# Pacing GpSimd's preparation steps by an estimate, and reordering the two products in each slot, in a fused attention and mixture kernel

## The chip, the cores and the metric

One core of one Trainium2 chip. The time is the device time of one execution in microseconds; the kernel before was run three times, with a median of 1210.46 us (1207.51 to 1210.76). The profile is of one more execution (1209.25 us by the same clock, 1207.5 us from its first to its last recorded instruction). TensorE's granted clock was full in it. All data are fp32.

## The reference: decayed linear attention, then four weighted two-layer experts

```python
# attention: batch 4, heads 8, seq 768, head_dim 64, in blocks of 64
for b in range(nb):
    qb, kb, vb = (q[:, :, sl], k[:, :, sl], v[:, :, sl])
    intra = np.einsum('bhic,bhjc->bhij', qb, kb) * Dmask[None]
    intra = np.einsum('bhij,bhjd->bhid', intra, vb)
    inter = np.einsum('bhid,bhde->bhie', qb * lam_pow[None], kv_state)
    out[:, :, sl] = intra + inter
    ...                                   # kv_state decays and takes in the block
# (B,H,S,D) -> x of (3072, 512); experts: E 4, F 1024
p = domain_probs / (domain_probs.sum(-1, keepdims=True) + 1e-09)
for e in range(E):
    h = np.maximum(x @ w1[e], 0.0)
    out += p[:, e:e + 1] * (h @ w2[e])
```

## The kernel before

Tokens come in 3 groups of 1024, each with 4 experts: 12 units (g, e). Both matrix products of a unit are done by a fast scheme with 7 outer products (`M1` to `M7`) in place of 8, and the first product x @ w1 by a second level of 7 inner products within each. The sums and differences of weight blocks (`S1` to `S4`) and of x blocks (`T1` to `T4`) that this needs are made ahead of time, mostly on GpSimd, stored in device memory (`w1_ops`, `x_ops`, `w2_sums`, `w2_ops`), and read back in the order of use. In the last group the second product is nested too (`nested_product`). While unit n does its second product, unit n+1 does its first product, and the attention of the next group is worked in between.

All instructions of all engines are issued in program order by this one Python program, and each engine runs its own in that order, waiting for data. SyncE (`nc.sync`) issues nearly all DMA transfers, also in order: a store that waits for its data holds back the loads behind it. So where in the program a preparation step, its store or a load is put decides what it can hold up. The preparation steps are closures in a list, taken one at a time:

```python
    chores, stores, older, made = [], [], [], set()

    def pump():
        for f in older:
            f()
        older[:] = stores
        stores.clear()
        if chores:
            chores.pop(0)()

    def until(what):
        while what not in made:
            pump()

    def inner(eng, what, to, blk, ops, at):          # 4 sums of 128x256, then their stores
        ...
            tt(eng, b[name], b[x], b[y], op)
        stores.append(lambda: (
            nc.sync.dma_start(out=to[:, 0], in_=blk[:, 0, 0:256]),
            nc.sync.dma_start(out=to[:, 1:5], in_=s[:]),
            nc.sync.dma_start(out=to[:, 5:7], in_=blk[:, 1].rearrange("p (a f) -> p a f", a=2)),
            made.add(what),
        ))

    def weight_steps(block, total, ready):           # block: loads; total: 2 sums of 128x512; ready: inner
        return [
            lambda: (block("A11", 0, 0), block("A21", 1, 0), block("A22", 1, 1)), nothing, nothing,
            lambda: ready("M1"),
            lambda: total("S1", "A21", "A22", ALU.add), lambda: ready("M5"),
            ...
        ]
```

The reads. `feed` fetches the operands of a first product (two buffers each), `feed2` the weights of a second product (a pool of six tiles, two for each product):

```python
    def feed(g, e, m):
        ...
        until(("x", g, m))
        until(("w1", e, m))
        xs = stream.tile([P, 7, 256], FP32, name="xs_in", tag="x")
        nc.sync.dma_start(out=xs[:], in_=x_ops[g, MS.index(m)])          # L633
        ws = stream.tile([P, 7, 256], FP32, name="ws_in", tag="w")
        nc.sync.dma_start(out=ws[:], in_=w1_ops[e, MS.index(m)])         # L635
        ...

    def first_product(g, e, m, blocks, tags):        # tags: PSUM banks g1, g3
        while (g, e, m) not in fed:
            pump()
        ...
        def inner(i):
            t = tags[0] if i in ("M1", "M6", "M5", "M3") else tags[1]
            ...
            for j in range(2):
                nc.tensor.matmul(...)                # L706: pg
            at, begins = READ[i]                     # then VectorE (or ScalarE) reads the bank
            ...
        return [lambda i=i: inner(i) for i in INNER] + [lambda: finished(g, e, m, blocks, new)]
        # INNER = ("M1", "M7", "M6", "M4", "M5", "M2", "M3")
```

`second_product` gives four parts (L760, tile q, each read by VectorE into `acc`) and a closing step; `nested_product` gives seven inner ones (L931, tile pq) and a closing step, with the pairs of banks q01/q02 and q11/q12 in turn. In the trace every matmul of the source stands as two matmul instructions.

The first expert's products on the first group are done directly (`direct_product`, L1021) with blocks still on chip, and the operands of the second expert's are made on the spot by `own(m)`: `own_x` on VectorE, `own_w1` on GpSimd, and a store of both (L1000). Then the main loop:

```python
    for at, (g, e) in enumerate(units):
        if (g, e) == (0, 1) or (g, e) == (0, 2):
            chores.extend(prepare_w2(e + 1) + prepare_w1((e + 2) % E))
        ...
        for i in range(7):
            for _ in range(2 if at + i == 0 else 1):
                if fill2:
                    feed2(*fill2.pop(0))
            ...
            if nested:
                order = [a[0:2], b[0:2], a[2:4], b[2:4], a[4:6], b[4:6], a[6:8], b[6:8]]
            else:
                order = [a[0:2], b[0:1], a[2:4], b[1:2], a[4:6], b[2:3], a[6:8], b[3:5]]
            for x, part in enumerate(order):         # a: first product of the next unit, b: second of this
                for f in part:
                    if f:
                        f()
                now[0] += 1
                ...
                if x == 0 and at * 7 + i >= 6 and fill:
                    feed(*fill.pop(0))
                ...                                  # at x 5 and some x 2: a step of the attention
                if x % (2 if g == 0 else 3) == 0:
                    pump()
```

## Time and profile before

| view | value |
|---|---|
| time, median of three runs | 1210.46 us |
| span of the profiled execution | 1207.5 us |
| TensorE matmul / weight load busy | 1187.3 / 1028.4 us |
| VectorE / ScalarE / GpSimd busy | 792.4 / 262.1 / 635.0 us |
| device memory traffic over the span | 262 GB/s |
| TensorE idle, 87 to 100 us | 2.95 us |
| TensorE idle, 400 to 896 us | 0.20 us |
| waits of SyncE for GpSimd, at L159 and L231 | 36.0 and 32.0 us |

Engines are called PE (TensorE matmul), PEld (its weight loads), DVE (VectorE), ACT (ScalarE), POOL (GpSimd) and SP (SyncE); SPq is the issuing of DMA by SyncE. "L706" is line 706 of the kernel; L94 is the helper that records every two-operand sum, so there the tile tells the sums apart. The chain that ended last is followed back from the last instruction, at each step to what released it. Matmul ends are modelled, so a short stall can stand inside "busy"; it then shows as a longer piece in the chain. A window's row gives its length, then for each engine the busy time and the number of instructions, then the clock, the DMA share and the rate.

### The profile page before, as it was taken

The page shows a single profiled execution, that of the slowest core. Times are in us where ns is not written, and L with a number is a line of the kernel's source. Part 1 is how long each engine was busy: PE and PEld are TensorE (multiplying, and loading weights), DVE is VectorE, ACT ScalarE, POOL GpSimd, SP SyncE. Part 2 cuts the span into 40 slices and gives each one's busy share as a digit, 9 for nine tenths or more (in the row PEclk, how much of TensorE's full clock was granted, in tenths as well). Part 3 has the DMA queues.
Part 4 walks back from the last instruction along what each step waited for, and adds up shares of the span by engine and source line. Part 5 has one row for each costly group of instructions (what it writes and reads, how often), then busy time and mean ns, then how long its engine had stood idle before and what let it go on. Part 6 is the DMA issues. An engine that isn't in the chain of part 4 may idle for free.

```text
span 1207.5 us, 17884 instructions
## 1 busy us (share of the span) xinstructions
PE 1187.3 (98%) x6593; PEld 1028.4 (85%) x6593; DVE 792.4 (66%) x1313; ACT 262.1 (22%) x476; POOL 635.0 (53%) x600
## 2 busy tenths in 40 slices
PE   7999999999999999999999999999999999999998
PEld 6887888888888888888888888888888888888877
DVE  5597687478467746746765774764665667777774
ACT  3322122112212211311221120120143241241132
POOL 4664258376366900025534746405665764873873
PEclk9999999999999999999999999999999999999999
DMA  9668479999999976679987998988987667566542
GB/s 234 186 217 293 171 250 330 366 332 349 334 328 344 306 233 197 225 238 291 299 284 239 298 326 309 304 311 259 320 297 249 226 216 260 205 248 211 203 172 72
DMA packets 227448, 317.94 MB, mean 263 GB/s; under 512 B 91649, under 2 KB 168865, under 8 KB 227361
## 3 DMA queue, kind: packets, MB, share of 16 engines
q1 hardware_dynamic: 219920, 314.63, 77.1%
q10 hardware_dynamic: 7440, 2.17, 0.8%
q8 instruction: 52, 0.85, 0.3%
q14 instruction: 36, 0.29, 0.1%
HBM read 231.40 MB, written 85.34 MB: 262 GB/s over the span
## 4 chain that ended last, share of the span: by engine, by line
PE 92%; DVE 3%; DMA 2%; SPq 2%; issue 1%; ACT 0%; DVEq 0%
PE pg L706 38%; PE q L760 30%; PE pq L931 13%; PE pM L1021 3%; PE op L488 2%; PE sp L460 2%; DMA ws_in<-w_ops 1%; PE op L483 1%; DVE m L94 1%; SPq L115 1%; PE kp L437 1%; PE qp L437 1%; PE op L496 1%; DVE hS L94 1%; PE pM L901 1%
## 5 line engine op out<-in xcount | busy, mean ns | idle before, releaser
L706 PE MATMUL pg<-xs_in,ws_in 128*128 128x256 f32 x1960 | 473.2, 382 | 1.4 <-DMA ws_in<-w_ops 1.0
L706 PEld LDWEIGHTS pg<-xs_in,ws_in 128*128 128x128 f32 x1960 | 368.7, 190 | 57.9 <-DVE m L94 5.7
L94 DVE TENSOR_TENSOR m<-pg,m 128x512 f32<-128x512 f32 x451 | 307.7, 688 | 132.2 <-PE pg L706 124.1
L760 PE MATMUL q<-w2t,hS 128*128 128x256 f32 x1024 | 242.6, 380 | 0.0
L760 PEld LDWEIGHTS q<-w2t,hS 128*128 128x128 f32 x1024 | 194.3, 190 | 26.3
L776 DVE SCALAR_TENSOR_TENSOR acc<-q,gate,acc 128x256 f32<-128x256 f32 x192 | 92.5, 482 | 155.8 <-PE q L760 155.5
L760 PE MATMUL q<-w2t,m 128*128 128x256 f32 x768 | 181.9, 380 | 2.1 <-DMA w2t<-in_moe_w_dram 2.1
L760 PEld LDWEIGHTS q<-w2t,m 128*128 128x128 f32 x768 | 145.7, 190 | 22.1 <-ACT m L1033 2.5
L718 ACT ACTIVATE m<-m 128x512 f32<-128x512 f32 x132 | 82.9, 630 | 346.7 <-DVE m L94 308.7
L94 POOL TENSOR_TENSOR kn<-kn,s_decay 128x512 f32<-128x512 f32 x20 | 22.6, 1132 | 204.1 <-PE kp L437 161.8
L94 POOL TENSOR_TENSOR m<-m,xT 128x512 f32<-128x512 f32 x64 | 81.2, 1286 | 73.9 <-ACT m L718 60.4
L94 DVE TENSOR_TENSOR sums<-pq,sums 128x256 f32<-128x256 f32 x154 | 64.6, 422 | 46.8 <-PE pq L931 43.1
L931 PE MATMUL pq<-acc,w2t 128*128 128x256 f32 x352 | 86.7, 380 | 0.0
L714 ACT COPY m<-pg 128x512 f32<-128x512 f32 x88 | 51.2, 585 | 142.9 <-PE pg L706 142.8
L94 DVE TENSOR_TENSOR m<-m,m 128x512 f32<-128x512 f32 x96 | 79.3, 832 | 0.0
L931 PEld LDWEIGHTS pq<-acc,w2t 128*128 128x128 f32 x352 | 66.9, 190 | 9.4 <-issue 0.6
L94 POOL TENSOR_TENSOR ops<-w2b 128x256 f32<-128x256 f32 x24 | 18.3, 783 | 104.2 <-DMA w2b<-in_moe_w_dram 92.9
L653 ACT ACTIVATE m<-m 128x512 f32<-128x512 f32 x48 | 30.3, 631 | 147.0 <-DVE m L94 147.0
L94 POOL TENSOR_TENSOR acc<-hT,hT 128x512 f32<-128x512 f32 x32 | 40.2, 1269 | 30.7 <-PE pq L931 21.3
L94 DVE TENSOR_TENSOR hS<-m,m 128x512 f32<-128x512 f32 x64 | 52.5, 824 | 5.6 <-ACT m L718 5.6
L94 POOL TENSOR_TENSOR w2o<-w2b 128x512 f32<-128x512 f32 x32 | 42.2, 1341 | 13.0 <-DMA w2b<-in_moe_w_dram 11.2
L94 POOL TENSOR_TENSOR acc<-hT,acc 128x512 f32<-128x512 f32 x32 | 40.7, 1270 | 7.4 <-PE pq L931 5.4
(126 smaller groups left out, 1321.1 us busy)
## 6 DMA issues: line engine op xcount, KB each, us to landing
xs_in<-x_ops SPq DMA_DIRECT2D x70, 896.0 KB, 4.9
ws_in<-w_ops SPq DMA_DIRECT2D x70, 896.0 KB, 8.2
w2t<-w_ops SPq DMA_DIRECT2D x66, 256.0 KB, 6.6
w2t<-w_sums SPq DMA_DIRECT2D x64, 256.0 KB, 5.0
w_ops<-ops SPq DMA_DIRECT2D x28, 512.0 KB, 5.7
w2t<-in_moe_w_dram SPq DMA_DIRECT2D x48, 256.0 KB, 4.2
x_ops<-ops SPq DMA_DIRECT2D x17, 512.0 KB, 6.2
w2b<-in_moe_w_dram SPq DMA_DIRECT2D x32, 256.0 KB, 5.7
```

Of the source, the lines that this page charges most:

```text
L94: eng.tensor_tensor(out=o, in0=a, in1=b, op=op)
L437: nc.tensor.transpose(out=x[:, ac * C:(ac + 1) * C], in_=y[:, 2 * ac:2 * ac + 2].rearrange("p r d -> p (r d)"), identity=ident[:],)
L460: nc.tensor.matmul(out=sp[r][:, ac * C:(ac + 1) * C], lhsT=hc(kT)[half[r], ac], rhs=hc(qT)[half[r], ac], start=True, stop=True,)
L488: nc.tensor.matmul(out=op[r][half[x], a * C:(a + 1) * C], lhsT=vn[:, 4 * r + 2 * a + x], rhs=hc(st[r])[:, 2 * a + x], start=(first and a = ...
L653: nc.scalar.activation(out=o[:], in_=o[:], func=AF.Relu)
L706: nc.tensor.matmul(out=p[:, j * 256:(j + 1) * 256], lhsT=ws[i][:, j * P:(j + 1) * P], rhs=xs[i], start=(fresh and j == 0), stop=True, skip ...
L714: nc.scalar.copy(out=new[at][:], in_=p[:])
L718: nc.scalar.activation(out=new[at][:], in_=new[at][:], func=AF.Relu)
L760: nc.tensor.matmul(out=p[:, s * DH:(s + 1) * DH], lhsT=h[A_OF[m]][:, c * 256 + s * P:c * 256 + (s + 1) * P], rhs=fed2[g, e, m][uu][:, c], ...
L776: nc.vector.scalar_tensor_tensor(out=o, in0=x, scalar=w, in1=o, op0=ALU.mult, op1=ALU.add)
L931: nc.tensor.matmul(out=p[:, 0:256], lhsT=fed3[e, m, x // 2][:, x % 2, c * P:(c + 1) * P], rhs=b[B_OF[i]][:, c * 256:(c + 1) * 256], start= ...
L1021: nc.tensor.matmul(out=p[:, s * 256:(s + 1) * 256], lhsT=a[c][:, f:f + P], rhs=b[:, c, j * 256:(j + 1) * 256], start=(s == 0 and c == 0), ...
```

## The change

It does four things. A running estimate of GpSimd's backlog is kept in slots (`now` counts slots, every sum on GpSimd adds its elements / 480), a preparation step begins when the estimate says that the last one has been worked off (`free`), and its store is put into SyncE's queue two slots after the estimate says that its sums are done, instead of two pumps later. The pump is called in every slot, with a factor for each group (`PACE`), and also in the prologue; where something must exist at once, steps are forced. Within a slot pair, the second product's part goes ahead of the first product's. And the weights of the first two second products are asked for before the last direct product; as that keeps the weights one outer product further ahead, each `feed2` later asks for the product after the next. Before the first chunk of a group overwrites the x tile, the x operands of the group before it are forced (`until`). Results have a list of their own and are stored at the next pump.

```diff
     def tt(eng, o, a, b, op):
         eng.tensor_tensor(out=o, in0=a, in1=b, op=op)
+        if eng is nc.gpsimd:
+            busy[0] = max(busy[0], now[0]) + math.prod(o.shape[1:]) / 480
+    now, busy, free = [0], [0.0], [0.0]
...
+    chores, queue, results, made = [], [], [], set()
+    LEFT = 1
+    def store(f):
+        queue.append((busy[0] + 2, f))
+    def pump(pace=1.0, force=False):
+        while results:
+            results.pop(0)()
+        begins = chores and (force or free[0] <= now[0])
+        while queue and (force or queue[0][0] <= now[0] or begins and len(queue) > LEFT):
+            queue.pop(0)[1]()
+        if begins:
+            begin = free[0] = max(free[0], now[0] - 1)
+            was = max(busy[0], now[0])
             chores.pop(0)()
+            free[0] = max(free[0], begin + max(pace * (busy[0] - was), 1))
+    def pause(n):
+        def step():
+            free[0] = max(free[0], now[0] + n)
+        return step
     def until(what):
         while what not in made:
-            pump()
+            pump(force=True)
...                                       # every stores.append(...) becomes store(...)
-            lambda: (block("A11", 0, 0), block("A21", 1, 0), block("A22", 1, 1)), nothing, nothing,
+            lambda: (block("A11", 0, 0), block("A21", 1, 0), block("A22", 1, 1)), pause(6),
...
             def end(n=n):
+                if n == g * CPG:
+                    for m in MS:
+                        until(("x", g - 1, m))
                 values(n, ("s0", "s1"))
...                                       # prologue: now[0] += 1; pump() after every part
+    chores.extend((*prepare_w2(1), *raws, pause(4), mine["M1"], sum_own("S1", "A21", "A22", ALU.add)))
     for m in SEQ0[2:]:
+        if m == SEQ0[-1]:
+            for _ in range(2):
+                feed2(*fill2.pop(0))
         for x, f in enumerate(direct_product(0, m, blocks, ("g1", "g3", "q01", "q02", "q11", "q12"))):
...
+    start, w1_steps = now[0], prepare_w1(2)
+    def pause_till(i, x):
+        def step():
+            free[0] = max(free[0], start + 8 * i + x)
+        return step
     chores.extend((
-        mine["M5"], sum_own("S2", "S1", "A11"), nothing, nothing,
-        mine["M6"], sum_own("S3", "A11", "A21"), nothing, nothing,
+        mine["M5"], sum_own("S2", "S1", "A11"),
+        pause_till(0, 4), mine["M6"], sum_own("S3", "A11", "A21"),
...                                       # M2, M7, M3, M4 likewise at (1, 4) to (4, 4)
+    PACE = 1.0, 1.4, 1.0
     for at, (g, e) in enumerate(units):
-        if (g, e) == (0, 1) or (g, e) == (0, 2):
-            chores.extend(prepare_w2(e + 1) + prepare_w1((e + 2) % E))
+        if at == 0:
+            chores.extend(prepare_w2(2) + prepare_w1(3) + prepare_w2(3) + prepare_w1(0))
...
-            for _ in range(2 if at + i == 0 else 1):
-                if fill2:
-                    feed2(*fill2.pop(0))
+            if fill2:
+                feed2(*fill2.pop(0))
...
-            if nested:
-                order = [a[0:2], b[0:2], a[2:4], b[2:4], a[4:6], b[4:6], a[6:8], b[6:8]]
+            if not ahead:
+                order = [[], b[0:2], [], b[2:4], [], b[4:6], [], b[6:8]]
+            elif nested:
+                order = [b[0:2], a[0:2], b[2:4], a[2:4], b[4:6], a[4:6], b[6:8], a[6:8]]
             else:
-                order = [a[0:2], b[0:1], a[2:4], b[1:2], a[4:6], b[2:3], a[6:8], b[3:5]]
+                order = [b[0:1], a[0:2], b[1:2], a[2:4], b[2:3], a[4:6], b[3:5], a[6:8]]
...
-                if x % (2 if g == 0 else 3) == 0:
-                    pump()
+                pump(PACE[g])
```

## The prediction

> **What bounds the kernel now.** I read the page first: the shares of the engines, then the windows of the trace, then the chain that ended last in the windows where TensorE was not full, then TensorE's waits.
>
> ```profile
> PE 1187.3 (98%) x6593; PEld 1028.4 (85%) x6593; DVE 792.4 (66%) x1313; ACT 262.1 (22%) x476; POOL 635.0 (53%) x600
> ```
>
> TensorE is the bound: idle 1207.5 - 1187.3 = 20.2 us in all. The next engine, VectorE, has 66%, GpSimd 53%. So the paced engine, GpSimd, isn't the limit; its work can only hurt by being late or by getting in the way of something. Where do the 20 us lie? The windows (length, then busy us of PE, PEld, DVE, ACT, POOL, clock, DMA share, GB/s) say:
>
> ```profile
> 87.00:100.00 13.00, 10.05 (x45) 7.97 (x44) 12.80 (x17) 4.40 (x8) 7.47 (x7) 1.00 0.55 195
> 165.00:175.00 10.00, 8.76 (x42) 7.39 (x40) 9.57 (x15) 1.89 (x3) 5.94 (x6) 1.00 0.55 191
> 217.00:259.00 42.00, 41.05 (x254) 34.99 (x253) 25.16 (x40) 5.85 (x11) 26.80 (x25) 1.00 0.97 342
> 400.00:896.00 496.00, 495.80 (x2668) 432.98 (x2667) 309.45 (x502) 92.45 (x162) 208.70 (x223) 1.00 0.84 278
> 896.00:1151.00 255.00, 254.78 (x1166) 220.05 (x1165) 174.74 (x310) 70.13 (x133) 169.54 (x136) 1.00 0.64 229
> ```
>
> The reader is to see that between 87 and 1151 us only 2.95 + 1.24 + 0.95 + 0.20 + 0.22 = 5.6 us are idle. The rest is before 60 us (6.0 in the first 20 us, 1.85 in the next 40) and after 1151 us (6.8 of the span); neither the first loads nor the closing additions are touched by the diff.
>
> The largest hole, at 93.7 to 99.1 us, is explained by the chain in order of time (start, us, what):
>
> ```profile
> 88.35 1.75 DVE ops L94 x2
> ...
> 91.85 0.33 SPq L1000
> ...
> 94.63 4.34 DMA w2t<-in_moe_w_dram
> 98.97 0.14 issue
> 99.11 1.10 PE q L760 x4
> ```
>
> VectorE makes the x operands of `own("M1")` until 91.8; SyncE's queue stands in order behind the store of them (L1000); only then the weights of the first second product are asked for, they land at 98.97, and TensorE starts L760 at 99.11. The direct products (L1021) ended at 93.7. From there to the end of that first L760 part, at 101.07, TensorE did 16 matmul instructions; eight take 1.73 us elsewhere in the chain, so 3.46 us of work took 7.4: **3.9 us lost**.
>
> A second loss is hidden in "busy". In the last group of tokens the chain shows, product after product, the same pattern:
>
> ```profile
> 929.76 0.86 PE pg L706 x4
> 930.62 0.86 PE pq L931 x4
> 931.49 1.92 PE pg L706 x8
> 933.40 1.73 PE pq L931 x8
> ```
>
> The eight L706 matmuls that open a product take 1.81 to 1.98 us, not 1.73. They write bank g1, which the last inner product (M3) of the product before also used, and VectorE must first empty it: 0.69 us for 128x512 from PSUM. Between the two stand only the 0.86 us of the half part of L931. TensorE's weight-load waits in 900 to 1150 us name it:
>
> ```profile
> PEld pg L706 <- DVE m L94: 4.9, 14, 0.6
> ```
>
> From 907.15 to 1140.23 us the chain has 19 such periods, mean 12.27 us; 56 instructions at 1.73/8 us would be 12.09. So 0.18 x 19 = **3.4 us** are lost there.
>
> **What the Trainium skill says.** "Perfetto Trace Analysis", section Identifying the Most-Contended Engine, warns that matmul busy is no measure of headroom, and points to the busy share of weight loads. This trace agrees: 98% against 85%, and the 3.4 us above are nearly invisible as idle time (0.22 us). The same page, Matmuls, wants independent groups to rotate through PSUM banks so that emptying one overlaps the next; here L931 rotates over pairs of banks and doesn't stall, while L706 returns to g1 and does. "GPSIMD Engine Reference", section 3.1, has 4497 ns for a two-input add of 2048 fp32 per partition; an estimate from that, a quarter, is 1.12 us for 512. The trace has 1.27 to 1.47 us for the 128x512 groups of GpSimd and 0.73 to 0.93 for 128x256. The measurement decides.
>
> **The change part by part.** One slot of the main loop: a product takes 12.95 us for 8 slots (711.18 to 724.13 in the chain), 1.62 us each.
>
> 1. *The estimate.* 512 elements / 480 = 1.07 slots = 1.73 us; 256 give 0.86 us. That is 20 to 35% above the measured 512 forms and about right for 256. So the pace is a little slower than GpSimd can go and should never pile work up.
> 2. *Pace.* Before, in group 0, a step every 2 slots; now one begins when the last is taken as done. A `ready` step has 4 x 256 and a `total` 2 x 512, both 1024/480 = 2.13 slots, against 2 before. In group 1: 1.4 x 2.13 = 3.0 against 8/3 = 2.67. Groups are thus paced much as before; pauses and plain loads are cheaper. Counting the queue through slot by slot, the deadlines hold: weights of expert 2, "M1", are stored about 10 slots ahead of the slot that asks for them, the last of expert 0 more than 50. The tight spots are the first two `own` steps (both forced just ahead of their product), the forced `until` at the fifth product of the first unit (about 8 slots of GpSimd work queued at once), and x of group 1, M5, forced by one step. I expect no TensorE idle time from this part, 0 +- 2 us.
> 3. *Stores by time, not two pumps later.* SyncE waited 36.0 us for GpSimd at L159 and 32.0 at L231, with the weights of the next product behind it. That caused TensorE's two waits for ws_in (1.0 us). Some of it goes: I take 0.5 us.
> 4. *First second-product weights asked for ahead.* The four w2t transfers now stand in SyncE's queue before the direct M4 and the `own("M1")` store. The 4.34 us of landing lie beside 7 us of L1021. The 2.09 us wait goes, and so do the 0.86 us (0.22 + 0.64) in which TensorE waits for VectorE to empty g1 and g3, since the L760 part now comes first. `own("M1")` also moves behind the direct M4 in VectorE's order, so its 3.5 us (88.3 to 91.8) no longer delay the emptying of the direct banks. But VectorE is 12.80 of 13.00 us busy there, and its backlog (the hS sums) must be worked off. Of 3.9 us I count 3.0.
> 5. *Second product first.* Cyclically the order of parts is the same, a b a b; what moves is the seam. Old: the last a (0.86), the last b, then the next a. In the last group that b was the half part, 0.86 us; new, the next product's full part, 1.73 us, lies between, longer than 0.69 us plus hand-over. So 3.0 of the 3.4 us go. b doesn't stall in its place, as it alternates banks, except at unit seams (three, 0.2 us each). In groups 0 and 1 the old gap was already 1.73 us: nothing. At the last seam (1151 us) the wait of 0.96 us before L931 at 1153.47 shrinks, since the last b now ends 0.86 us earlier: 0.7 us.
> 6. *VectorE's pile at 165 to 175 us* (1.24 us): the x operands of M4 move from slot 0 of the sixth product to slot 5 of the fifth, beside the attention values. Half, 0.6 us.
> 7. *Against:* the second product reads the last relu of the unit before one slot earlier (6 us behind the matmul instead of 9.5; needed 0.69 + 0.63 plus queue), a full w2 pool of six tiles so that SyncE waits for TensorE there, and the forced steps. I put 1 us.
>
> Sum: 0.5 + 3.0 + 3.0 - 0.6 + 0.7 + 0.6 - 1.0 = **6.2 us**. From the median of the runs before, 1210.5: **1204.3 us**.
>
> **The rivals.**
> A. *VectorE takes over.* The two early holes are VectorE's piles (12.80 of 13.00 and 9.57 of 10.00 us busy); taking away the w2t wait lets TensorE run into the emptying of g1 a product later. For: the shares. Against: in 100 to 165 us VectorE is only 44.4 of 65 busy, it catches up fast. Then only the 3 us of the seams remain: 1207.
> B. *Transfers collide.* The DMA share is 0.97 to 0.99 from 217 to 400 us, and ws_in lands in 7.9 to 11.3 us there with a product of 12.95 us as its slack. The w2t of the product after next now waits for TensorE and goes out together with xs_in and ws_in. If each product of this stretch (about 13) waited 0.5 us: +6.5, a total of 1210. Against: bytes and issues per product are the same, and ws_in had 1.6 us or more to spare.
> C. *Forced steps stall TensorE.* If the `until` before the values of chunk 8 puts 8 slots of GpSimd work ahead of something TensorE needs, a hole of up to 10 us appears once: 1213. Against: the x operands are made by VectorE, and the next product's weights by GpSimd are due 16 slots later.
>
> **Range and chances.** Faster by over 2% needs 24 us; only 9 us between 87 and 1151 us are there to be had, so 1%. Slower by over 2% needs a new repeating stall, which I can't find in the slots: 2%. If all goes well 1200; if B and C both hit 1214. I take 1197.5 to 1211.
>
> **What would show it.** Right: no wait of L760 for w2t near 94 us, L1021 followed directly by L760; periods near 12.09 us in the last group with no eight-instruction L706 piece above 1.75; SyncE's waits for GpSimd far lower; TensorE busy about the same, idle about 15 us. Wrong: waits of L706 for ws_in or for VectorE's m that grow in 94 to 400 us, or a hole about the fifth product of the first unit.

## The result: 0.3% faster, and the profile after

| | median, us | lowest to highest | ratio to before (95% interval) |
|---|---|---|---|
| before | 1210.0 (6 runs) | 1207.51 to 1211.75 | 1 |
| after | 1205.76 (6 runs) | 1205.51 to 1207.41 | 0.9971 [0.9957, 0.9984] |

The change takes 4.2 us off, 0.3%, which counts as the same within 2%. The forecast was 6.2 us and 1204.3. The profiled execution of after spans 1205.6 us, 1183.2 of them with TensorE busy, so 22.4 us idle: not fewer than before (20.2), but more. Yet the kernel is faster; 2.5 us of idle time more than before lie in the first 60 us of this execution. First, then, the windows of the trace of after (start and end, length, busy us of PE, PEld, DVE, ACT, POOL, granted clock, DMA share, GB/s), the same five stretches as before:

```profile
87.00:100.00 13.00, 11.64 (x55) 9.95 (x54) 12.90 (x18) 5.04 (x9) 10.59 (x8) 1.00 0.31 75
165.00:175.00 10.00, 10.00 (x48) 8.81 (x47) 9.59 (x17) 3.15 (x5) 6.90 (x6) 1.00 0.56 222
217.00:259.00 42.00, 42.00 (x258) 36.29 (x257) 26.57 (x43) 4.95 (x10) 22.83 (x23) 1.00 0.98 348
400.00:896.00 496.00, 494.96 (x2662) 430.67 (x2661) 305.75 (x499) 91.84 (x162) 214.66 (x227) 1.00 0.86 281
896.00:1151.00 255.00, 253.89 (x1171) 221.54 (x1169) 177.99 (x313) 70.12 (x133) 164.51 (x132) 1.00 0.64 234
```

The hole in the first row is halved (1.36 us idle, before 2.95). The second and third rows have none left (before 1.24 and 0.95). The last two rows have more idle time than before, 1.04 and 1.11 us against 0.20 and 0.22. In the last group that says little, since what was lost there was hidden in long matmuls. TensorE's weight-load waits between 900 and 1150 us show it better; columns are total us, how often, longest:

```profile
PEld pg L725 <- DVE m L95: 1.3, 2, 0.7
```

Before it was 4.9 us in 14 waits. Against that, three waits of L950 have come in, of 1.7 us in all. (The lines of after have new numbers: L725 is the first product, L779 the plain second product, L950 the nested one, L1035 the direct one, L760 the request for w2t, L652 and L654 those for xs_in and ws_in, L95 the helper that adds.) The chain of after shows the eight-instruction pieces at 1.73 us each:

```profile
927.63 0.86 PE pq L950 x4
928.50 0.86 PE pg L725 x4
929.36 1.73 PE pq L950 x8
931.09 1.73 PE pg L725 x8
...
939.72 0.86 PE pq L950 x4
```

One period is 939.72 - 927.63 = 12.09 us, the figure that eight in 1.73 us give.

**Where the time went.** To compare two traces I cut them at the same number of issued TensorE instructions, so that each stage holds the same amount of work. The start (58.2 to 61.1 us, with the first loads) differs by up to 3.0 us between executions, by 1.1 us between two of one kernel; nothing is concluded from it. Units are counted from 0, the main loop's first; "products" in the table are those of unit 0, and "row one" below is the table's first row. "Best" is the ninth experiment.

| stage, us | before | after | after, again | best |
|---|---|---|---|---|
| last 5 direct products and product 1 of the main loop | 51.25 | 49.16 | 48.63 | 47.89 |
| products 2 to 4 | 41.02 | 41.38 | 41.38 | 41.38 |
| products 5 and 6 | 30.57 | 29.24 | 29.24 | 29.24 |
| unit 1 | 106.65 | 105.22 | 105.22 | 105.22 |
| units 2 and 3 | 208.26 | 209.63 | 208.58 | 209.33 |
| unit 5 | 97.06 | 97.31 | 97.33 | 96.92 |
| units 8 to 10 (last group) | 258.57 | 256.15 | 256.15 | 255.20 |
| last unit, to its last TensorE instruction | 50.12 | 52.66 | 52.66 | 52.86 |

Product 7 and units 4, 6 and 7 agree within 0.02 us in these four. Two more kernels (experiments 6 and 10) issue the same program as after until the last group; over all four executions the first row is 48.28 to 49.16 (mean 48.62) and units 2 and 3 are 208.38 to 209.63 (mean 208.92). A difference of a few tenths in those rows, from one trace each, is therefore not evidence. The last two rows need care: the cut between them falls on the last unit's first matmul, and the change moves a wait from one side of it to the other (see the seam below). Without that, units 8 to 10 gained 1.5 us and the seam lost 1.6.

### The profile page after: what moved, and what is told of

The parts are those of the page before. It is cut to its first block, busy times and chain, and to the rows that moved or that the text cites. A ratio compares the mean times of both kernels' runs of the same rounds, so it can differ in the third digit from the quotient of the medians.

```text
span 1205.6 us, 17838 instructions
## 1 busy us (share of the span) xinstructions
PE 1183.2 (98%) x6593; PEld 1025.9 (85%) x6593; DVE 789.7 (66%) x1313; ACT 262.0 (22%) x476; POOL 634.2 (53%) x600
## 4 chain that ended last, share of the span: by engine, by line
PE 92%; DVE 2%; DMA 2%; SPq 2%; issue 1%; ACT 0%; POOL 0%; DVEq 0%
PE pg L725 37%; PE q L779 31%; PE pq L950 12%; PE pM L1035 3%; PE sp L476 2%; PE op L504 2%; DMA ws_in<-w_ops 1%; DVE m L95 1%; PE op L499 1%; SPq L122 1%; PE qp L453 1%; PE kp L453 1%; PE op L512 1%; PE pM L920 1%; SPq L341 1%
## 5 line engine op out<-in xcount | busy, mean ns | idle before, releaser
L725 PE MATMUL pg<-xs_in,ws_in 128*128 128x256 f32 x1960 | 470.4, 380 | 1.6 <-DMA ws_in<-w_ops 1.0
L725 PEld LDWEIGHTS pg<-xs_in,ws_in 128*128 128x128 f32 x1960 | 370.5, 190 | 55.0 <-DVE m L95 2.5
L95 DVE TENSOR_TENSOR m<-pg,m 128x512 f32<-128x512 f32 x451 | 308.0, 687 | 112.2 <-PE pg L725 102.0
L779 PE MATMUL q<-w2t,hS 128*128 128x256 f32 x1024 | 243.3, 380 | 0.0
L779 PEld LDWEIGHTS q<-w2t,hS 128*128 128x128 f32 x1024 | 192.9, 190 | 26.8 <-issue 0.3
L779 PE MATMUL q<-w2t,m 128*128 128x256 f32 x768 | 182.5, 380 | 0.0
L779 PEld LDWEIGHTS q<-w2t,m 128*128 128x128 f32 x768 | 144.7, 190 | 20.1 <-issue 0.2
L95 POOL TENSOR_TENSOR m<-m,xT 128x512 f32<-128x512 f32 x64 | 81.5, 1289 | 78.4 <-ACT m L737 61.1
L95 POOL TENSOR_TENSOR kn<-kn,s_decay 128x512 f32<-128x512 f32 x20 | 22.0, 1101 | 179.6 <-PE kp L453 150.7
L95 DVE TENSOR_TENSOR sums<-pq,sums 128x256 f32<-128x256 f32 x154 | 64.1, 421 | 49.1 <-PE pq L950 41.5
L950 PE MATMUL pq<-acc,w2t 128*128 128x256 f32 x352 | 86.7, 379 | 1.9 <-POOL acc L95 1.9
L95 DVE TENSOR_TENSOR m<-m,m 128x512 f32<-128x512 f32 x96 | 80.0, 838 | 0.0
L950 PEld LDWEIGHTS pq<-acc,w2t 128*128 128x128 f32 x352 | 66.8, 190 | 11.3 <-issue 2.2
L95 POOL TENSOR_TENSOR ops<-w2b 128x256 f32<-128x256 f32 x24 | 17.4, 745 | 108.0 <-DMA w2b<-in_moe_w_dram 108.0
L95 DVE TENSOR_TENSOR hS<-m,m 128x512 f32<-128x512 f32 x64 | 53.2, 835 | 8.4 <-ACT m L737 8.4
L95 POOL TENSOR_TENSOR w2o<-w2b 128x512 f32<-128x512 f32 x32 | 42.5, 1349 | 29.1 <-DMA w2b<-in_moe_w_dram 24.6
L95 POOL TENSOR_TENSOR acc<-hT,hT 128x512 f32<-128x512 f32 x32 | 40.1, 1270 | 32.5 <-DVE hT L95 19.6
L95 POOL TENSOR_TENSOR acc<-hT,acc 128x512 f32<-128x512 f32 x32 | 40.7, 1272 | 5.0 <-PE pq L950 2.7
```

Of the source, the lines that this page charges most:

```text
L95: eng.tensor_tensor(out=o, in0=a, in1=b, op=op)
L725: nc.tensor.matmul(out=p[:, j * 256:(j + 1) * 256], lhsT=ws[i][:, j * P:(j + 1) * P], rhs=xs[i], start=(fresh and j == 0), stop=True, skip ...
L779: nc.tensor.matmul(out=p[:, s * DH:(s + 1) * DH], lhsT=h[A_OF[m]][:, c * 256 + s * P:c * 256 + (s + 1) * P], rhs=fed2[g, e, m][uu][:, c], ...
L950: nc.tensor.matmul(out=p[:, 0:256], lhsT=fed3[e, m, x // 2][:, x % 2, c * P:(c + 1) * P], rhs=b[B_OF[i]][:, c * 256:(c + 1) * 256], start= ...
```

## What each remaining wait of after is

**The first hole.** No wait for w2t is left. What came in its place, in the chain of after:

```profile
95.55 1.08 DVE hS L95
...
98.22 0.42 DVE ops L95
98.64 0.14 issue
98.77 1.10 PE pg L725 x4
```

The first product now waits 1.36 us for the x operands that `own("M1")` has VectorE make. They stand at the end of VectorE's pile of hS and m sums, which was there before too. But the pile has grown slower (the first form below took 946 ns on average in before, with GpSimd busy 7.47 us of the window). Groups by form in 87 to 100 us (operation, shapes, count, busy us, mean ns), first VectorE and one GpSimd group of after:

```profile
L95 DVE TENSOR_TENSOR hS<-m,m 128x512 f32<-128x512 f32 x4 | 4.1, 1050 | 0.0
L95 DVE TENSOR_TENSOR m<-pM,m 128x512 f32<-128x512 f32 x5 | 3.4, 679 | 0.0
L95 POOL TENSOR_TENSOR w1o<-w1b 128x512 f32<-128x512 f32 x2 | 3.0, 1502 | 5.9 <-issue 5.9
```

and VectorE's same two forms in the fourth experiment, where the weights are not asked for early and GpSimd is busy 4.60 of these 13 us instead of 10.59:

```profile
L95 DVE TENSOR_TENSOR hS<-m,m 128x512 f32<-128x512 f32 x6 | 4.9, 830 | 0.0
L95 DVE TENSOR_TENSOR m<-pM,m 128x512 f32<-128x512 f32 x4 | 2.7, 678 | 0.0
```

The sum of two SBUF tensors takes 1050 ns on average beside GpSimd and 830 with less of it. The sum with one input in PSUM takes 679 and 678. "SBUF — State Buffer", section "SBUF: two separate sides", says that a two-SBUF-input VectorE operation and a GpSimd operation that reads SBUF take one port pair by turns, the loser blocked. This trace agrees in direction: the one form stretches, the other does not (single sums of it range from 0.68 us, even beside a 128x256 sum of GpSimd, which then took 1.13 us instead of 0.73, to 1.7). GpSimd works there because the early w2t requests stand ahead of the raw w1 blocks in SyncE's queue, so that those go out later (the last pair at 80.8 us, in the fourth experiment at 74.3).

**Unit 3.** One `until` step forces all queued stores out. In this profile SyncE first waits for a w2t tile to come free (until 402.07), and the last piece of the store of an x operand behind it goes out late, when an earlier load has landed:

```profile
405.61 5.79 DMA x_ops<-xo
...
411.85 8.61 DMA ws_in<-w_ops
420.46 0.14 issue
420.60 1.97 PE pg L725 x8
```

GpSimd had been done at 396.5; the store landed at 411.39; only then could the block be read back, and TensorE waited 0.81 us for the weights behind it. In the second execution of after the request for ws_in went out 0.4 us earlier (411.45), the load took 0.1 us less, and the wait was 0.22 us.

**The seam before the last unit** costs most. TensorE's timeline of after there (start, length, what, idle time before and its releaser):

```profile
1148.02 1.03 PE L725 MATMUL pg<-xs_in,ws_in 128*128 128x256 f32 x4
1149.08 1.10 PE L950 MATMUL pq<-m,w2t 128*128 128x256 f32 x4
1150.02 1.03 PE L950 MATMUL pq<-acc,w2t 128*128 128x256 f32 x4
1152.90 2.83 PE L950 MATMUL pq<-acc,w2t 128*128 128x256 f32 x12 [1.85 <-POOL acc L95]
```

and VectorE's in the same stretch:

```profile
1149.30 0.69 DVE L95 TENSOR_TENSOR hT<-hp,m 128x512 f32<-128x512 f32 x1 [0.32 <-POOL m L95]
1149.91 0.68 DVE L95 TENSOR_TENSOR m<-pg,m 128x512 f32<-128x512 f32 x1
1150.51 0.68 DVE L95 TENSOR_TENSOR hT<-hp,hT 128x512 f32<-128x512 f32 x1
1151.77 0.69 DVE L95 TENSOR_TENSOR hT<-hp,m 128x512 f32<-128x512 f32 x1 [0.58 <-ACT hp L603]
1152.38 0.74 DVE L95 TENSOR_TENSOR sums<-pq,sums 128x256 f32<-128x256 f32 x2
```

The last part of the last first product (L725, 1148.02) is now the last thing in its unit. Its values go through VectorE (m, 1149.91), ScalarE (relu, then the copy hp, to 1151.7) and VectorE again (hT, 1151.77). Only behind that, in VectorE's order, stands the reading of the banks (`sums`) that the last unit wants to write again. TensorE has two inner products left to do meanwhile, and before it had a second-product part more. The profile names GpSimd's `acc` as the releaser, which ended at 1152.89. Two later kernels (9 and 12) decide between the two: in the three, TensorE goes on 0.10 us after the first `sums` ends each time, but 0.01, 0.00 and 0.36 us after `acc`. So it is VectorE's reading.

TensorE's timeline of before at the same place:

```profile
1150.62 1.03 PE L706 MATMUL pg<-xs_in,ws_in 128*128 128x256 f32 x4
1151.48 1.03 PE L931 MATMUL pq<-hT,w2t 128*128 128x256 f32 x4
1153.47 1.10 PE L931 MATMUL pq<-m,w2t 128*128 128x256 f32 x4 [0.96 <-ACT m L718]
```

Here the wait stands ahead of the last unit's first matmul, and so in units 8 to 10 of the table; in after it stands behind its eighth, in the last unit. Counted as time over the 0.22 us from one matmul to the next, before waits 1.12 us ahead of the last unit and 0.07 behind its eighth matmul; after waits 0.19 and 2.01. So 0.93 us of the change in both rows is a wait that changed sides. The other 0.6 us of the loss come later: at 1160.25 TensorE waits 1.23 us for a bank that VectorE reads only behind three hT sums, where before it was 0.64 us, behind two.

## The experiments

All ratios are to the kernel before, measured beside it.

### 1 and 2: the new order alone, the early weights alone

```diff
-    order = [a[0:2], b[0:1], a[2:4], b[1:2], ...]      # kernel 1: before, with only this
+    order = [b[0:1], a[0:2], b[1:2], a[2:4], ...]
```
```diff
+        if m == SEQ0[-1]:                              # kernel 2: before, with only this
+            for _ in range(2):
+                feed2(*fill2.pop(0))
```

> The kernel before with the new order of parts alone. Theory (the seam and the late weights are two separate losses): in the last group the product's period falls from 12.27 to 12.09 us, about 2 us net for the 21 products there because of new waits where two units meet; but the first L760 part now stands ahead of the two L706 parts that used to fill the time until the weights land at 99 us, so the hole at 94 us grows by 1.5 us. Sum: 0 to 1.5 us faster than before, about 1209. Rival (the order is what the gain of the whole change comes from): 1206.

> The kernel before with the first two weights asked for ahead of the last direct product and nothing else. Theory: the wait of 2.09 us of L760 for w2t at 99 us goes, and the two L706 parts still wait for their banks (0.86 us), so the piece from the end of the direct products to the end of the first L760 part falls from 7.4 to about 5 us: 2.5 us faster, 1207.5. Rival (VectorE's pile takes over): the piece stays at 6.5 us or more and the total is within 1 us of before.

Kernel 1: 1216.32 us, ratio 1.0047 [1.0031, 1.0063]; the expectation missed. Units 8 to 10 were 256.48 us, so the order's gain in the last group is there (2.1 us, 1.2 without the wait that changed sides); the last unit was 52.67, so the loss at the seam also comes with the order alone. The rest was lost at the first hole (row one 55.41) and in products 5 and 6 (32.70). In the old order L706's first part filled some of the wait for w2t; now L760 comes first and all of it lies bare. Chain of kernel 1, then the window behind the hole:

```profile
95.09 3.77 DMA w2t<-in_moe_w_dram
98.85 0.14 issue
98.99 3.75 PE q L760 x8
102.74 2.15 PE pg L706 x8
```

```profile
99.00:103.00 4.00, 4.00 (x10) 3.19 (x11) 0.70 (x2) 0.00 (x0) 0.00 (x0) 0.50 1.10 287
```

After 5.4 us without work, eight matmuls took 3.75 us and the next eight 2.15, instead of 1.73: the granted clock was 0.50 for 4 us. "TensorE: Matmul & The Clock Gate", Part 1, says that an idle window of some 3.4 us, in a row of windows that run on whatever the kernel does, halves the clock until a busy one has passed. This run agrees; but the length of the hole alone doesn't decide, as the 2.3 us hole of experiment 4 left the clock at 1.00 and one of 2.1 us in experiment 6 did not. The hole here thus cost 5.4 us and 2.4 more behind it.

Kernel 2: 1209.55 us, 0.9985 [0.9976, 0.9994]. Row one was 49.87, 1.4 us below before, so the early request alone is worth less than half of the 3.0 us of the forecast's step 4, and less than the 2.5 expected here.

### 3 to 5: the change without one part or with one part only

Kernel 3 is the changed kernel with the old order, kernel 4 without the early request (and so with weights asked for one product ahead), kernel 5 with neither: the pacing alone, with the forced steps and the separate list of results that belong to it.

> The changed kernel with the old order of parts. Theory: the last group is back at 12.27 us for a product (257 us in all instead of 255.8), the last seam at 1151 us is back at 55.2 us from there to the end instead of 56.7, the first hole is as in the changed kernel or a little shorter. Sum: 0 to 1.5 us slower than the changed kernel, about 1206.5. Rival (the order carries the gain): 1209.

> The changed kernel with the first weights asked for at the start of the main loop again, two at once. Theory: the four w2t transfers stand behind the stores of own M1 that are waiting for VectorE, later than in the kernel before because that VectorE work now comes behind the direct products; L760 comes first and waits until about 103 us: 4 to 6 us slower than the changed kernel, 1210 to 1212. Rival (w2t was hidden anyway): within 1 us of the changed kernel. As each feed2 then asks one product ahead again, the waits of SyncE for L760 (140 us) go too; if these had cost anything, the stretch from 182 to 895 us gets shorter than 713 us.

> The changed kernel with the old order of parts and the first weights asked for as before: the pacing alone. Theory (asking two products ahead fills the pool of six w2 tiles, so SyncE waits for L760 ahead of the loads of xs_in and ws_in; with the old order L760's last part ends after L706's, which makes these loads late): here the weights are one product ahead again, so the third and fourth units, which took 106.4 and 105.6 us in the changed kernel with the old order alone, go back to 104.5 and 105. The wait of L760 for w2t at 99 us is gone although nothing is asked for early, because the store of own M1 now stands behind the weights. In all about 1209, 1 to 2 us faster than before. Rival (the pacing itself makes the reads late, not the full pool): third and fourth unit stay above 105.5 and the total is 1211.

| | median, us | ratio | row one | products 5, 6 | unit 1 | units 2, 3 | units 8 to 10 | last unit |
|---|---|---|---|---|---|---|---|---|
| 3, old order | 1211.66 | 1.0009 [0.9999, 1.0019] | 50.14 | 29.06 | 106.10 | 212.02 | 258.33 | 50.12 |
| 4, no early request | 1208.16 | 0.9976 [0.9967, 0.9985] | 48.11 | 31.74 | 105.28 | 209.25 | 257.77 | 52.67 |
| 5, pacing alone | 1210.97 | 0.9995 [0.9982, 1.0008] | 49.47 | 29.06 | 105.22 | 207.94 | 258.65 | 50.12 |

Kernel 3 was expected at 1206.5 us and kernel 4 at 1210 to 1212; both missed. Kernel 5 did in units 2 and 3 what was expected, but its total was to be 1209. What follows:
- The pacing alone brings the 1.4 us of unit 1 and the 1.5 us of products 5 and 6, and most of row one. It puts the store of `own("M1")` behind the weights in SyncE's queue. A wait of 2.4 us for VectorE's hT sums appears in unit 7 (93.18 us, elsewhere 90.65); why only there isn't settled. It doesn't explain why the median hardly moves: the profiled execution has it and took 1207.60 us, at a mean clock of 1.000. Eight of the twelve executions had a mean clock of 0.996 to 0.998 and took 1211.8 us on average; where the clock fell in them no trace shows.
- The early request isn't what fills the first hole: without it row one is *shorter*, 48.11. What it buys is the second product ahead, which the new order needs (kernel 5, with the old order, has 29.06 us in products 5 and 6 without it). In kernel 4 the store of another `own` product holds SyncE up from 165 to 170 us, other loads follow until 174.5, and in the chain the weights come too late:

```profile
174.64 4.70 DMA w2t<-in_moe_w_dram
179.35 0.04 issue
179.39 1.78 PE q L779 x7
```

- Old order, pacing and weights two products ahead don't go together: 212.02 us in units 2 and 3 of kernel 3, against 207.94 with weights one product ahead (kernel 5) and 208.92 with the new order. In kernel 3 SyncE waits for the second product's last part to free a w2t tile, which in the old order ends after the first product's, and the requests for xs_in and ws_in stand behind it. That is not the whole cause: kernel 2, two products ahead in the old order but without the pacing, has as long a wait of SyncE for w2t tiles (174.0 us in all, kernel 3 166.4), and took 208.40. What the pacing adds isn't settled.
- The last unit is 50.12 with the old order and 52.66 to 52.67 with the new one, in every pairing with pacing and early weights up to here; without the wait that changed sides, that is a loss of 1.6 us.

### 6 and 10: banks that alternate across units

In after the last product of a unit and the first of the next both use q01/q02.

```diff
-    [i % (2 if ahead else 3)]
+    [(at + i) % 2 if ahead else (i + 1) % 3]           # kernel 6
+    [(at + i + 1) % 2 if ahead else i % 3]             # kernel 10
```

> The changed kernel, but in the last group the pairs of banks q01/q02 and q11/q12 alternate across the units as well; before, the last product of a unit and the first of the next used the same pair. Theory: the waits where two units meet (0.78 us near 976, 0.27 near 1063 us, part of the last one) were due to the banks and go; units 8 to 10 together fall by about 0.8 us, the last by up to 0.5: 1 us faster than the changed kernel, 1204.8. Rival (VectorE and ScalarE are late there whatever the bank): no change in these units.

> The changed kernel with the alternating pairs of banks alone, shifted by one so that the last unit begins with q01/q02 as it does in the changed kernel. Theory (at the seams TensorE waits for a pair whose sums are not yet read; in the first form the gain was given back because the last unit's own rotation was changed): units 8 to 10 together 255.2 us instead of 256.15, last unit 52.7 us or less, total 0.9 us under the changed kernel. Rival (the last unit is long because VectorE and GpSimd are late there, and a TensorE that arrives 0.9 us earlier waits 0.9 us longer): units 8 to 10 255.2 us, last unit 53.6 us, total the same as the changed kernel.

Kernel 6: 1206.64 us, 0.9962 [0.9947, 0.9978]. Units 8 to 10 took 255.20 us (-0.95), the last unit 54.67 (+2.0). Kernel 10, with the last unit's own rotation as it was: 1205.88 us, 0.9954 [0.9943, 0.9965], units 8 to 10 again 255.2, last unit 52.86. The seam's wait in the timeline of after,

```profile
978.22 1.13 PE L950 MATMUL pq<-m,w2t 128*128 128x256 f32 x4 [0.51 <-ACT sums L958]
```

is gone in kernel 10, where the same four matmuls start at 977.22 with no idle time ahead of them.

The rival, that TensorE merely arrives earlier at the last seam and waits longer there, would have made the last unit 53.6; it falls. But the theory's other half, that kernel 6 lost its gain by the pairs of its last unit, isn't shown. Its profile has TensorE at half clock there; two windows of kernel 6:

```profile
1147.59:1151.00 3.41, 1.29 (x6) 0.85 (x5) 2.83 (x6) 2.22 (x4) 3.33 (x4) 1.00 0.86 335
1151.00:1154.41 3.41, 3.41 (x9) 2.69 (x8) 1.56 (x4) 0.00 (x0) 3.12 (x3) 0.50 0.46 193
```

Half of 3.41 us is 1.7 of the 1.8 us by which its last unit is longer than that of kernel 10, which has the same hole of 2.1 us (1149.67 to 1151.79) at full clock. Against the changed kernel beside it (1206.57) the gain is 0.7 us, as large as the stages say (0.95 - 0.20), but inside the scatter of the medians.

### 7: no lag before a store

```diff
-        queue.append((busy[0] + 2, f))
+        queue.append((busy[0], f))
```

> The changed kernel with stores put into SyncE's queue as soon as the estimate says the sums are done, not two slots later. Theory: the store of x of group 1, M5, goes out earlier, so the two waits for ws_in near 406 and 420 us (1.0 us) go and the fourth unit falls from 105.3 to about 104.2; SyncE's waits for GpSimd rise from some 46 us towards the 68 of the kernel before, without reaching TensorE: 0.5 to 1 us faster than the changed kernel. Rival (the lag protects SyncE's queue): ws_in is late in several places, 1 to 3 us slower.

1205.12 us, 0.9955 [0.9939, 0.9971]. Unit 3 fell to 103.81. Together with experiments 9 and 12, which have this edit too, it is 103.81 three times; the six kernels with the new order, pacing and the lag (after twice, 4, 6, 8, 10) have 104.06 to 105.52. But unit 2 took 104.81, 105.52 and 106.24 in the three, and 104.31 to 104.33 in the six. The sum of the two units is 209.33 on average without the lag (208.62 to 210.05) and 209.13 with it (208.38 to 209.84): **no gain shown, only moved**. SyncE's timeline shows why, first in experiment 12, then in the second execution of after:

```profile
299.60 0.47 SPq L175 DMA_DIRECT2D w_ops<-w1b  x1
300.16 0.38 SPq L176 DMA_DIRECT2D w_ops<-ops  x1
300.58 0.50 SPq L177 DMA_DIRECT2D w_ops<-w1b  x1
301.18 2.27 SPq L760 DMA_DIRECT2D w2t<-w_sums  x2
303.54 0.42 SPq L652 DMA_DIRECT2D xs_in<-x_ops  x1
304.01 0.42 SPq L654 DMA_DIRECT2D ws_in<-w_ops  x1
```

and here, with the store only behind the loads:

```profile
301.13 0.89 SPq L760 DMA_DIRECT2D w2t<-w_sums  x2
302.11 0.38 SPq L652 DMA_DIRECT2D xs_in<-x_ops  x1
302.54 0.42 SPq L654 DMA_DIRECT2D ws_in<-w_ops  x1
```

Without the lag a store of 1.5 us of issue slips ahead of the loads, ws_in is asked for 1.5 us later and takes 9.93 us, and TensorE waits 1.7 us for it. The DMA share is 0.96 to 1.00 there.

### 8: two products ahead, but only from the third product on

```diff
-        if m == SEQ0[-1]: ...                          # the early request is left out
+            for _ in range(2 if at + i == 0 or (at, i) == (0, 2) else 1):
```

> The changed kernel without the early request, but with two products' weights asked for at once in the third product, so that they are two ahead from there on. Theory: the early request is not what fills the first hole; it only pushes the loads of w1 of expert 1 back, so that GpSimd works beside VectorE at 87 to 98 us and slows it. So direct products and first product together take 48.1 us as in the kernel without the early request (49.2 in the changed one), while the wait of 2.3 us for w2t near 177 us, which that kernel had, is gone (fifth and sixth product 29.2, not 31.7): 1 us faster than the changed kernel, 1204.8. Rival (the early request counts): no gain or slower.

1205.39 us, 0.9958 [0.9943, 0.9973]. Row one 48.12 and products 5 and 6 29.24: both gains at once. So what the early request was good for is the look-ahead, and the place where it was put cost 0.5 us (48.12 against the mean of 48.62; with pacing and new order, row one is 47.89 to 48.12 in the four kernels without it and 48.28 to 49.16 in the five traces with it).

### 9, 11 and 12: the fixes together, after again, and the seam

Kernel 9 joins experiments 7, 8 and 10. Kernel 11 is the changed kernel once more. Kernel 12 is kernel 9 with the old order in the last product of unit 10 alone:

```diff
+            elif at == len(units) - 2 and i == 6:
+                order = [a[0:2], b[0:2], a[2:4], b[2:4], a[4:6], b[4:6], a[6:8], b[6:8]]
```

> The changed kernel with its three fixes together: a store may go as soon as its estimated step is done (no lag of 2 slots), the weights of a second product are asked for two products ahead only from the third product on (instead of before the last direct product), and in the last group the pairs of banks alternate across units, so that the last product of a unit and the first of the next never share one. If the three losses are separate, they add: about 1.0 us at the first hole, 1.5 us in unit 3 and 0.9 us at the seams of units 8 to 10, with the last unit no longer than the 52.7 us it has in the changed kernel because its own pairs are as there. That is about 3.4 us under the changed kernel: about 1202.3 us, ratio to the kernel before 0.9935. Rival (what is taken away at one seam comes back at the next wait, as with the first form of the banks): within 1.5 us of the changed kernel, ratio 0.996.

> The changed kernel again, beside the others on the same chip: 1205.5 us, ratio 0.9965, with unit 3 at 105.3 us and the last unit at 52.7 us as in its first profile. If the differences of 0.3 us between stages of two kernels mean anything, every stage after the first 60 us repeats within 0.1 us.

> The kernel with the three fixes, and the old order (first product's part ahead of the second's) in one product alone, the last of unit 10. Theory (the last unit is 2.5 us longer than before because, with the new order, the last first-product values come one part later and the VectorE and GpSimd work behind them with it, so that the reading of the first bank of the last unit is late): the last unit falls back to 50.1 us, unit 10 grows by up to 0.9 us where two parts of the first product meet, total 1.6 to 2.5 us under the kernel with the three fixes. Rival (the last unit's length comes from the whole last group's order, for instance VectorE's backlog): the last unit stays within 0.5 us of that kernel's.

Kernel 9: 1204.1 us (1203.68 to 1204.22), 0.9941 [0.9928, 0.9953]. Kernel 11: 1206.57, 0.9959 [0.9947, 0.9971]. Kernel 12: 1203.86, 0.9941 [0.9929, 0.9953]. Kernel 9 beats the changed kernel beside it by 2.5 us; 3.4 were expected. The losses don't simply add: 0.7 at row one and 0.95 in units 8 to 10 came, the 1.5 of unit 3 did not (see 7). The claim of kernel 11's expectation that stages repeat within 0.1 us holds for most and fails for row one (0.53 off) and unit 3 (1.05 off), those that hang on transfers.

Kernel 12 moves the last unit from 52.86 to 51.49, and unit 10 from 85.28 to 86.33, where two first-product parts now meet. Against the 50.1 us of the old order this looks like half of the loss, but there the cut hides a wait. Counted as at the seam above, the wait behind the eighth matmul falls from 2.28 us in kernel 9 to 0.92, below the 1.2 of before, so the place of that first-product part does set it, as the theory has it. The later wait of 1.23 us, behind three hT sums of VectorE, stays. Paying for the move in unit 10 leaves 0.3 us, within the scatter. The kernel before had the same sum of unit 10 and last unit 1.0 to 1.3 us lower (136.87); a seam without either cost wasn't found.

## Why the prediction was about right, and which terms were off

The total was near (6.2 us forecast, 4.2 measured), and TensorE stayed the bound. That a sum of terms of which one has the wrong sign comes out so near is in part luck: losses left out and gains put too low made up for each other. Step by step, with the change of each stage (mean of the like executions where there are several):

| step of the prediction | forecast | measured |
|---|---|---|
| 4: first second-product weights ahead | -3.0 | -2.63 in row one, but mostly by the pacing |
| 5: second product first, last group with its seams | -3.0 + 0.6 | -1.5 in units 8 to 10 (-2.42 as cut) |
| 5: the last seam | -0.7 | **+1.6** (+2.54 as cut) |
| 3: stores by time | -0.5 | -1.43 in unit 1 |
| 6: VectorE's pile at 165 to 175 us | -0.6 | -1.33 in products 5 and 6 |
| 2 and 7: forced steps and the rest | +1.0, step 2 none | +0.36 in products 2 to 4, +0.66 in units 2 and 3, +0.57 in unit 5 |
| sum | -6.2 | -3.7 by the stages, -4.2 by the medians |

- **The step that failed is the last seam of step 5.** It reasoned that the last b ends 0.86 us earlier and so the wait shrinks. The sign was wrong: it looked at when the second product's part ends and not at what the last unit needs, the last part of the *first* product, which the new order puts last. Experiment 1 (order alone) and 3 and 5 (old order) show that the loss comes with the order, at 1.6 us. This one term, 2.3 us off, is as large as the whole error (2.0 us by the medians, 2.5 by the stages).
- **Step 5 in the last group was right in mechanism**: 14 weight-load waits became 2, and periods are 12.09 us; the 3.6 us of waits at the openings of products in units 8 to 10 of before are gone, for 3.0 forecast. But 2.1 us of new waits, not 0.6, stand against them: 0.77 and 0.27 us at the two unit seams near 978 and 1064 us, and 0.53 us each in the sixth products of units 9 and 10, where the first product waits for VectorE's m.
- **Step 4 had the size roughly but the cause wrong.** Its own listing named the pacing's part (the `own("M1")` operands move behind the direct M4) as an aside; experiment 4 shows that to be the main thing. The early request by itself brings 1.4 us on the kernel before and takes 0.5 on the paced one. Rival A, VectorE taking over, is the wait that is left (1.36 and, in the second execution, 0.8 us).
- **Steps 3 and 6 were too small.** In step 3, I halved a wait of 1.0 us; it went wholly, and unit 1 gained 1.4. In step 6 I took half of the pile's 1.24 us; all of it went. Pacing alone shows both.
- **Step 2's "no idle time" was wrong** and rival C half right: a forced step does cost, 0.15 to 1.6 us in unit 3 over the six kernels with the lag, not at the fifth product of the first unit. SyncE there waits for a w2t tile, which step 7 had named. Rival B, transfers colliding, costs at most the same 0.7 us on average in units 2 and 3, not 6.5; with the old order and the pacing it would have cost 4 us there (experiment 3). The 0.36 us of products 2 to 4 come with the order alone too (experiment 1, 41.38 us), so the table's row isn't forced steps throughout; unit 5's 0.3 to 0.9 us was not looked into.
- Of the signs named beforehand, the missing wait for w2t, the periods and SyncE's shorter waits for GpSimd came true; the last, in SyncE's waits of after:

```profile
SPq L760 <- PE q L779: 140.2, 63, 9.4
SPq L248 <- POOL w2o L95: 29.2, 9, 5.9
SPq L176 <- POOL ops L95: 16.9, 7, 5.9
```

Waits for the first-product weights' sums fell from 36.0 to 16.9 us, those for w2_sums only from 32.0 to 29.2, and SyncE now waits 140 us for TensorE to free w2t tiles. "Idle about 15 us" failed (22.4), as the losses hidden in long matmuls had never counted as idle, the new ones at 98 and 1151 us do, and the first 60 us had 2.5 us more.

## What to carry to other kernels

When two interleaved streams swap places, go to the seam where one of them ends and ask which part the next stage needs first: a swap that frees a wait in every period can put the needed part last. A queue that issues in order turns "earlier" into "ahead of something", so an earlier store or load is worth testing against what then stands behind it, and the stages on both sides have to be summed. The same holds where a reordering moves a wait across the line between two stages: count the waits themselves. And repeat the trace of one kernel before reading tenths out of a stage.

## What the hardware showed that was not expected

- TensorE's granted clock fell to 0.50 in the midst of three of the traces: after a hole of 5.4 us (experiment 1), after one of 2.1 (experiment 6), and within one of 2.8 us (experiment 11, from 25.4 us on). Holes of 2.3 us (experiment 4), 3.0 (after, from 22.8 us) and 3.3 us (experiment 10, from 22.7 us) left it at 1.00. What parts them is how much work is left in the stretch of 3.41 us that ends where the clock changes: it held 0.36, 1.29 and 1.04 us of TensorE work in these three. The low clock then lasted 3.41 us, and twice that in experiment 1, whose next stretch held 1.05 us. Counting such stretches on from the first change of the clock in each trace, none of the others up to 1195 us held less than 1.47 us. So the same hole can cost nothing or 1.7 us, by where it falls.
- Of the 47 executions of the kernel before beside experiments 1 to 4, the nine with a mean clock of 1.000 took 1209.29 us on average, the six with 0.997 or less 1213.8: part of the scatter of the medians goes with the clock.
- VectorE's 128x512 sum of two SBUF tensors went from some 680 ns to means of 830, 946 and 1050 ns the more GpSimd worked beside it (4.60, 7.47 and 10.59 us of 13), while the sum with one PSUM input stayed at 678 to 679.
